# Forget attention and two MLPs on one core: the first eight attention units turn their probabilities by a product with a diagonal of the sums' reciprocals instead of normalising and transposing them

## The chip, the cores and the metric

The kernel runs on one core of a Trainium2 chip. The metric is the device time of one execution in microseconds (us); the median of the runs of the kernel before is 1039.59 us. TensorE is PE in the profile (PEld is its loading of weights), VectorE is DVE, ScalarE is ACT, GpSimd is POOL, and SP issues most of the DMAs.

## The reference

Inputs are q, k, v of shape (4, 8, 576, 64) and gates s of shape (4, 8, 576), all float32. What is computed, cut to what matters:

```python
scores = scale * np.matmul(q, k.transpose(0, 1, 3, 2))
cum = np.cumsum(np.maximum(s, 0.0), axis=-1)
bias = -(cum[:, :, :, None] - cum[:, :, None, :])
scores = np.where(causal, -1000000000.0, scores + np.minimum(bias, 0.0))
attn = np.exp(scores - np.max(scores, axis=-1, keepdims=True))
attn = attn / (np.sum(attn, axis=-1, keepdims=True) + 1e-09)
out = np.matmul(attn, v)                    # 4 x 8 x 576 x 64
x = out.transpose(0, 2, 1, 3).reshape(2304, 512)
h = x @ w_in;  r = max(h, 0);  x = (s * r * r + b) @ w_out         # first MLP, 512 -> 2048 -> 512
h = x @ w_in2; x = (max(h, 0) + alpha * min(h, 0)) @ w_out2        # second MLP
```

## The kernel before

The attention is cut into 32 units: a batch, a pair of heads, and a range of queries. A unit of range 0 has queries 0 to 320 in three blocks of 64, 128 and 128 rows (numbers 0, 1, 2); a unit of range 1 has queries 320 to 576 in two blocks of 128 (3, 4). The order is batch, range, pair, so units 0 to 3 are batch 0, range 0, and units 4 to 7 are batch 0, range 1. Names carry batch, pair and range: `sc_3_0_0_0_1` is a score of unit (0, 0, 1), which is unit 4.

For each head of a unit, `scores` (L402) makes the biased scores of each block, takes the row maximum (L459), and lets ACT do the exponential with the row sums `sm` (L471). Then DVE adds 1e-9 to the sums and takes reciprocals (L478, L479), and POOL multiplies each block's probabilities by them, in place (L482). `values` then turns the probabilities: for every 128 keys and every block that reaches them PE transposes a 128x128 piece into a PSUM bank `pt` (L513), 6 pieces for a head of range 0 and 9 for one of range 1. ACT or DVE copies the bank into SBUF (`pf`, L517), PE multiplies it with v (`av`, L529), and ACT copies the result into the MLP's input (`xf`, L544).

The first eight units are `native`: their scores and value products run in plain float32, where one product is two PE records over its columns. Later units split each operand in two and use the faster fp32r type.

The first MLP runs in seven blocks of 256 tokens and one of 512, each of 16 steps over slices of the hidden size: `up` (L781), ReLU and square on ACT (L800, L802), a split into a high part by ACT and a low part by POOL or DVE (L130, L131), and `down` (L895). Block 0 needs the outputs of units 0 to 3, block 1 those of units 4 to 7. So the program has an early stage, in which units 0 to 3 run with weight slices that are fetched and converted beside them (L140 to L142, L130, L131; `wt`, `w`), and PE fills gaps with products of a zero tile (`busy`, L97), and then a stage in which the units are interleaved with the MLP's steps. After the first MLP comes the second.

The order on each engine is not written by hand: a scheduler places every instruction when the program is built, by its own estimate of durations, and each engine then runs its list in order. Tiles of one tag share a slot; a new tile of that tag waits until the slot's last reader is done. The tags `xs0` and `xs1` have one slot each, and before the change unit 8 is the first to use them.

Of the kernel before, what the change touches and what calls it, by code (L numbers as in the profile page):

```python
# [8 lines left out]
F32 = mybir.dt.float32  # L9
# [3 lines left out]
AF = mybir.ActivationFunctionType  # L13
ALU = mybir.AluOpType
# [5 lines left out]
def tile_forget_attention__then__two_mlps(  # L20
# [20 lines left out]
    nc = tc.nc  # L41
    B, H, S, D = q.shape
    NT, DM = out.shape
    DFF = w_in1.shape[1] // 2
    P = 128
    NP = H // 2
# [5 lines left out]
    IB = [(0, 64)] + [(64 + 128 * n, 192 + 128 * n) for n in range(4)]  # L52
    R1 = IB[2][1]
    QK = S - R1 + S
    EARLY, NATIVE = NP, 2 * NP

# [8 lines left out]
    one = ctx.enter_context(tc.tile_pool(name="one", bufs=1))  # L67
# [12 lines left out]
    ident = const.tile([P, P], F32, name="ident")  # L80
# [13 lines left out]
    def busy(n):  # L94

        for _ in range(n):
            tc.keep_in_program_order(nc.tensor.matmul(scratch, dense[:, :P], dense, start=True, stop=True))  # L97
# [31 lines left out]
    def split(hi, lo, src, lo_eng=nc.vector):  # L129
        nc.scalar.copy(hi, src)  # L130
        lo_eng.tensor_tensor(out=lo, in0=src, in1=hi.bitcast(F32), op=ALU.subtract)  # L131
# [36 lines left out]
    for f in range(len(SPARE), NF):  # L168
        at = int((f - len(SPARE)) * PACE)
# [106 lines left out]
    class Unit:  # L276
        def __init__(self, n):
            self.n = n
            self.b, self.pr, self.rng = units[n]
            self.tag = "_".join(str(i) for i in units[n])  # L280
            self.h0 = 2 * self.pr
            self.blocks = (0, 1, 2) if self.rng == 0 else (3, 4)
            self.q0, self.q1 = (0, R1) if self.rng == 0 else (R1, S)
            self.nv = 3 if self.rng == 0 else 4
            self.probs = [None, None]

            self.early = 0 < n < EARLY
            self.native = n < NATIVE
            self.n_banks = 0
            self.cums = []  # L290

# [110 lines left out]
    def scores(u, h):  # L402

        own = HALF[h]
        head = u.b * H + u.h0 + h
        flip = u.native and h == 1
        nr = len(u.blocks)
        nm = two.tile([P, 3], F32, tag="nm", name=f"nm_{u.tag}_{h}")
        sm = two.tile([P, 3], F32, tag="sm", name=f"sm_{u.tag}_{h}")
        if u.rng == 0:  # L410
            nc.gpsimd.memset(sm[:, 0:1], 1.0)
        big = None if u.early else two.tile([P, 1088], F32, tag="probs", name=f"probs_{u.tag}_{h}")
        probs, col = {}, 0
        for r in u.blocks:
            i0, i1 = IB[r]
            rows = i1 - i0
            if u.early and r != 1:
                big, col = u.buf(two, 0, F32, "", f"probs{h}{r}"), 0

            width = -(-i1 // P) * P if i1 < S else S  # L420
            pt = probs[r] = big[:, col : col + width]
            col += width
            if width > i1:
                nc.gpsimd.memset(pt[:, i1:], 0.0)
            if r == 0:
                nc.gpsimd.memset(pt[64:P, 0:64], 0.0)

            if flip:
                nc.scalar.activation(
                    pt[:rows, :i1], u.cums[h][:rows, :i1], AF.Relu, scale=-1.0, bias=cumT[:rows, r, head : head + 1]  # L430
                )
            else:
                nc.vector.tensor_scalar(
                    out=pt[:rows, :i1], in0=u.cums[h][:rows, :i1], scalar1=cumT[:rows, r, head : head + 1],
                    scalar2=0.0, op0=ALU.subtract, op1=ALU.min,
                )
            nc.gpsimd.affine_select(
                out=pt[:rows, i0:i1], in_=pt[:rows, i0:i1], pattern=[[-1, rows]], base=0,
                channel_multiplier=1, compare_op=ALU.is_ge,
                fill=-MASKED if flip else MASKED,  # L440
            )
        u.probs[h] = probs
        for m, r in enumerate(u.blocks):
            i0, i1 = IB[r]
            rows, n = i1 - i0, i1
            a0 = i0 - u.q0
            pt = probs[r]
            init = -KEEP_ALL if flip else KEEP_ALL
            for j0, j1 in ([(0, n)] if n <= 512 else [(0, 320), (320, n)]):
                sc = u.bank("sc", f"sc{h}_{r}_{j0}")  # L450

                scr, all_ = sc[:rows, : j1 - j0], sc[:, : j1 - j0]
                aq = slice(a0, a0 + P)
                if u.native:
                    nc.tensor.matmul(all_, u.qk[0][own, aq], u.qk[1][own, j0:j1], start=True, stop=True)
                else:
                    nc.tensor.matmul(all_, u.xs[h][0][:, aq], u.xs[h][1][:, j0:j1], start=True, stop=False)
                    nc.tensor.matmul(all_, u.ql[h][:, aq], u.xs[h][1][:, j0:j1], start=False, stop=True)  # L458
                nc.vector.tensor_tensor_reduce(  # L459
                    out=pt[:rows, j0:j1], in0=scr, in1=pt[:rows, j0:j1], scale=SCALE if flip else -SCALE, scalar=init,  # L460
                    op0=ALU.subtract if flip else ALU.add, op1=ALU.max if flip else ALU.min,
                    accum_out=nm[:rows, m : m + 1],
                )
                if u.n < EARLY:
                    busy(1)
                init = nm[:rows, m : m + 1]
            if flip:
                nc.vector.tensor_scalar(
                    out=nm[:rows, m : m + 1], in0=nm[:rows, m : m + 1], scalar1=-1.0, scalar2=None, op0=ALU.mult
                )  # L470
            nc.scalar.activation(  # L471
                pt[:rows, :n], pt[:rows, :n], AF.Exp, bias=nm[:rows, m : m + 1], scale=1.0 if flip else -1.0,
                accum_out=sm[:rows, m : m + 1],
            )
            yield
        if u.n == 0:
            busy(4)
        nc.vector.tensor_scalar(out=sm[:, :nr], in0=sm[:, :nr], scalar1=1e-9, scalar2=None, op0=ALU.add)  # L478
        nc.vector.reciprocal(sm[:, :nr], sm[:, :nr])  # L479
        for m, r in enumerate(u.blocks):  # L480
            rows, n = IB[r][1] - IB[r][0], IB[r][1]
            nc.gpsimd.tensor_scalar(  # L482
                out=probs[r][:rows, :n], in0=probs[r][:rows, :n], scalar1=sm[:rows, m : m + 1],
                scalar2=1.0, op0=ALU.mult, op1=ALU.mult,
            )
        yield

    def values(u, h):
# [10 lines left out]
        for n_bank, bank in enumerate(banks):  # L499
            f0, fn = bank[0][1], bank[-1][1] + width[bank[-1][0]]  # L500
            tp = u.bank("tr", f"pt{h}_{n_bank}")
            moves = []
            for c, off in bank:
                for r in u.blocks:
                    i0, i1 = IB[r]
                    if P * c >= i1:
                        continue

                    partial = r and P * c > i0
                    o = off + i0 - max(q0, P * c)  # L510
                    moves.append((not partial, -c if partial else o, o, r, min(P * c, S - P)))
            for _, _, o, r, k0 in sorted(moves):
                nc.tensor.transpose(tp[:, o : o + P], u.probs[h][r][:, k0 : k0 + P], ident)  # L513
            n_p = (2 * h + n_bank) % 2
            if u.native:
                pf = two.tile([P, 512], F32, tag=("ph", "pl")[n_p], name=f"pf_{u.tag}_{h}_{n_bank}")
                (nc.scalar.copy, nc.vector.tensor_copy)[n_p](pf[:, f0:fn], tp[:, f0:fn])  # L517
                parts = (pf,)
            else:
                ph = two.tile([P, 512], F32R, tag="ph", name=f"ph_{u.tag}_{h}_{n_bank}")  # L520
                pl = two.tile([P, 512], F32R, tag="pl", name=f"pl_{u.tag}_{h}_{n_bank}")
                split(ph[:, f0:fn], pl[:, f0:fn], tp[:, f0:fn])
                parts = (ph, pl)
            yield
            for z, part in enumerate(parts):
                for c, o in bank:
                    w = width[c]
                    lhs = (u.vn if u.native else u.vs[h])[:, c].rearrange("p z d -> p (z d)")
                    nc.tensor.matmul(  # L529
                        av[:, nq - w : nq], lhs, part[:, o : o + w],  # L530
                        start=(c == 0 and z == 0), stop=(c == last_c and z == len(parts) - 1),
                        skip_group_check=True,
                    )
# [451 lines left out]
    for n in range(len(BLOCKS) * NF):  # L985
# [20 lines left out]
        for j in range(NF):  # L1006
            at = LAG[0] + int((j - len(SPARE)) * PACE) if j >= len(SPARE) else j
# [46 lines left out]
```

## Time and profile before

| | us |
|---|---|
| median of three runs | 1039.59 |
| the three runs | 1043.21, 1039.59, 1036.9 |
| profiled execution, its own time | 1039.36 |
| profiled execution, span from first to last instruction | 1037.6 |
| first MLP product (`up`, L781) starts at | 58.68 |

The profiled execution spent 1.76 us outside its span. The rows from it stand below; times in them count from the span's start. A busy PE in such a row includes the tails of pipelined matmuls, so that PE's speed is read from the distance between starts. A group's mean mixes undisturbed and delayed instructions.

### The profile page before, as it was taken

Reading aid. Unit: us, or ns where it says so; the run is one execution under the profiler, and the core shown is the slowest. Engines: PE = TensorE matmul, PEld = TensorE weight load, DVE = VectorE, ACT = ScalarE, POOL = GpSimd, SP = SyncE. Lnnn points to the kernel's source line nnn. Section 1 sums busy time; section 2 is a strip of 40 time slices with the busy share of each in tenths; the row PEclk is TensorE's granted clock in tenths of the full one; section 3 lists DMA queues with packets and bytes.
Section 4 is the critical chain, followed back from the end, with each engine's and each line's share of the span. In section 5 each row is a group of like instructions: output and inputs, shape, how many; then the busy total and the mean of one; then the engine's idle time right before and its main releaser. Section 6 shows DMA issues by size and latency. Waiting matters only on the chain. (4 is left out here: it accounts for less than half of the span.)

```text
span 1037.6 us, 20643 instructions
## 1 busy us (share of the span) xinstructions
PE 1018.5 (98%) x6949; PEld 925.5 (89%) x6952; DVE 674.4 (65%) x1605; ACT 670.7 (65%) x1668; POOL 450.6 (43%) x876
## 2 busy tenths in 40 slices
PE   9999999999999999999999999999999999999997
PEld 4578899999999999999999888888999999999996
DVE  6899665687677766677655865857665456455443
ACT  5878766777787877878776776645554454445433
POOL 5555675666677576777562000574611011001000
PEclk9899999999999999999999999999999999999999
DMA  7997443343143432324215762645644335334331
GB/s 150 257 249 223 120 76 68 73 98 76 40 89 67 99 72 52 82 65 91 68 34 177 230 199 78 205 148 176 200 154 142 102 114 171 103 102 133 105 102 48
DMA packets 197930, 125.45 MB, mean 121 GB/s; under 512 B 138496, under 2 KB 167936, under 8 KB 197824
## 3 DMA queue, kind: packets, MB, share of 16 engines
q1 hardware_dynamic: 193744, 123.56, 42.8%
q8 instruction: 55, 0.90, 0.4%
q10 hardware_dynamic: 4080, 0.57, 0.3%
q14 instruction: 51, 0.42, 0.1%
HBM read 106.19 MB, written 17.90 MB: 120 GB/s over the span
## 5 line engine op out<-in xcount | busy, mean ns | idle before, releaser
L781 PE MATMUL hp<-xh,w 128*128 128x256 f32 (+1 forms) x1024 | 229.9, 301 | 1.1 <-ACT r L800 1.1
L905 PE MATMUL acc<-w,ring 128*128 128x512 f32 x864 | 214.6, 392 | 1.1 <-DVE ring L131 0.7
L905 PEld LDWEIGHTS acc<-w,ring 128*128 128x128 f32 x864 | 155.9, 188 | 29.4 <-DVE ring L131 1.1
L781 PEld LDWEIGHTS hp<-xh,w 128*128 128x128 f32 x1024 | 171.4, 189 | 9.3 <-ACT r L800 1.4
L895 PE MATMUL acc<-gh,w 128*128 128x256 f32 x896 | 170.3, 286 | 0.4 <-ACT res L924 0.4
L781 PE MATMUL hp<-xl,w 128*128 128x256 f32 (+1 forms) x512 | 152.3, 298 | 0.0
L895 PEld LDWEIGHTS acc<-gh,w 128*128 128x128 f32 x896 | 135.3, 189 | 2.4 <-ACT res L924 1.0
L881 POOL TENSOR_TENSOR cc<-u,t 128x256 f32<-128x256 f32 x32 | 26.9, 839 | 237.2 <-DVE u L872 202.9
L895 PE MATMUL acc<-gl,w 128*128 128x256 f32 x448 | 117.7, 288 | 1.4 <-POOL gl L131 1.4
L482 POOL TENSOR_SCALAR probs<-probs,sm 64x64 f32<-64x64 f32 (+4 forms) x160 | 89.2, 571 | 58.9 <-DVE sm L479 51.9
L471 ACT ACTIVATE probs<-probs,nm 64x64 f32<-64x64 f32 (+4 forms) x160 | 89.9, 562 | 35.8 <-DVE nm L459 26.9
L131 POOL TENSOR_TENSOR gl<-r,gh 128x256 fp32r<-128x256 f32 x112 | 87.7, 784 | 51.3 <-ACT gh L130 41.4
L815 PE MATMUL p<-xs,sums 128*128 128x256 f32 x768 | 104.6, 282 | 0.4 <-DVE u L857 0.4
L815 PEld LDWEIGHTS p<-xs,sums 128*128 128x128 f32 x768 | 98.0, 189 | 2.0 <-DVE u L857 0.6
L781 PEld LDWEIGHTS hp<-xl,w 128*128 128x128 f32 x512 | 97.1, 190 | 2.7
L459 DVE CUSTOM_DVE_ANT_0 probs<-sc,probs 128x320 f32<-128x320 f32 (+3 forms) x160 | 68.4, 428 | 42.1 <-PE sc L458 28.8
L815 PEld LDWEIGHTS p<-xs,w 128*128 128x128 f32 x576 | 79.0, 189 | 8.4 <-DVE u L872 1.7
L800 ACT ACTIVATE r<-hp 128x256 f32<-128x256 f32 (+1 forms) x144 | 58.0, 403 | 43.7 <-PE hp L781 31.6
L815 PE MATMUL p<-xs,w 128*128 128x256 f32 x576 | 82.0, 282 | 2.3 <-DVE u L872 1.5
L895 PEld LDWEIGHTS acc<-gl,w 128*128 128x128 f32 x448 | 79.8, 189 | 2.5 <-POOL gl L131 1.9
L513 PE MATMUL pt<-ident,probs 128*128 128x128 f32 x480 | 75.3, 275 | 3.1 <-POOL probs L482 2.7
L826 DVE SCALAR_TENSOR_TENSOR ph<-pl,misc,ph 128x512 f32<-128x512 f32 x64 | 50.6, 790 | 42.3 <-ACT pl L842 42.3
(151 smaller groups left out, 2104.3 us busy)
## 6 DMA issues: line engine op xcount, KB each, us to landing
sums<-sums_d SPq DMA_DIRECT2D x128, 256.0 KB, 2.7
wi<-in_moe_w_in_dram SPq DMA_DIRECT2D x32, 512.0 KB, 5.0
wo<-in_moe_w_out_dram SPq DMA_DIRECT2D x32, 512.0 KB, 5.1
cum<-cum_d SPq DMA_DIRECT2D x32, 288.0 KB, 3.6
sums_d<-w SPq DMA_DIRECT2D x64, 128.0 KB, 1.9
cum<-cum_d SPq DMA_DIRECT2D x30, 160.0 KB, 3.0
nat<-in_k_dram SPq DMA_DIRECT2D x64, 72.0 KB, 2.5
x_d<-res SPq DMA_DIRECT2D x18, 256.0 KB, 2.4
```

Source lines behind the costliest of these rows:

```text
L131: lo_eng.tensor_tensor(out=lo, in0=src, in1=hi.bitcast(F32), op=ALU.subtract)
L459: nc.vector.tensor_tensor_reduce(out=pt[:rows, j0:j1], in0=scr, in1=pt[:rows, j0:j1], scale=SCALE if flip else -SCALE, scalar=init, op0=AL ...
L471: nc.scalar.activation(pt[:rows, :n], pt[:rows, :n], AF.Exp, bias=nm[:rows, m : m + 1], scale=1.0 if flip else -1.0, accum_out=sm[:rows, m ...
L482: nc.gpsimd.tensor_scalar(out=probs[r][:rows, :n], in0=probs[r][:rows, :n], scalar1=sm[:rows, m : m + 1], scalar2=1.0, op0=ALU.mult, op1=A ...
L513: nc.tensor.transpose(tp[:, o : o + P], u.probs[h][r][:, k0 : k0 + P], ident)
L781: nc.tensor.matmul(hs, a[:, c], b[c], start=(n == 0), stop=(n == len(terms) * NCC - 1))
L800: relus.append(nc.scalar.activation(r, hs, AF.Relu, scale=1.0 / W_SCALE).ins)
L815: nc.tensor.matmul(bank, lhs[:, c * P : (c + 1) * P], rhs[:, c], start=(start and c == 0 and z == 0), stop=(c == 1 and z == 2), skip_group ...
L826: nc.vector.scalar_tensor_tensor(out=r, in0=u, scalar=nalpha[:, f : f + 1], in1=r, op0=ALU.mult, op1=ALU.add).ins
L881: nc.gpsimd.tensor_tensor(out=cc[:, T:], in0=u3, in1=t5, op=ALU.add)
L895: nc.tensor.matmul(banks[d] if count == 2 else acc[d // 2][:, d % 2], a[:, d * P : (d + 1) * P], b, start=(f == 0 and (d % 2 == 0 or count ...
L905: nc.tensor.matmul(banks[m], a[:, m * P : (m + 1) * P], b, start=(f == 0 and b is woh and a is gh), stop=(f == NF - 1 and a is gl),)
```

## The change

For units 0 to 7 the pass of L482 is gone. In its place a 128x128 float32 diagonal of the reciprocals is made for each block, in a tile of the tag `xs0` (first head, made by ACT: the identity times the row's reciprocal) or `xs1` (second head, made by DVE). The transposition becomes an ordinary float32 product of the probabilities, as weights, with that diagonal, as the moving operand, which turns and scales at once. Its columns are cut to those that are needed: 64, 128, 128, 64, 128 and 64 for a head of range 0 (576 in all), and seven times 128 and twice 64 for a head of range 1 (1024). A clearing of 64 rows of block 0 on POOL (L426) falls away too. Units 8 to 31 are as before.

```diff
-    EARLY, NATIVE = NP, 2 * NP
+    EARLY, NATIVE, SPREAD = NP, 2 * NP, 8
...
+            self.spread = n < SPREAD
+            self.diag = [None, None]
...
-            if r == 0:
+            if r == 0 and not u.spread:
                 nc.gpsimd.memset(pt[64:P, 0:64], 0.0)
...
+        if u.spread:
+            u.diag[h] = one.tile([P, QK], F32, tag=f"xs{h}", name=f"diag{h}_{u.tag}")
         for m, r in enumerate(u.blocks):
             rows, n = IB[r][1] - IB[r][0], IB[r][1]
+            if u.spread:
+                turn = u.diag[h][:rows, m * P : m * P + rows]
+                if h:
+                    nc.vector.tensor_scalar(
+                        out=turn, in0=ident[:rows, :rows], scalar1=sm[:rows, m : m + 1], scalar2=None, op0=ALU.mult
+                    )
+                else:
+                    nc.scalar.activation(turn, ident[:rows, :rows], AF.Copy, scale=sm[:rows, m : m + 1])
+                continue
             nc.gpsimd.tensor_scalar(
...
-            for _, _, o, r, k0 in sorted(moves):
+                    moves.append((not partial, -c if partial else o, o, r, min(P * c, S - P), max(0, P * c - i0)))
+            for _, _, o, r, k0, skip in sorted(moves):
+                if u.spread:
+                    rows = IB[r][1] - IB[r][0]
+                    at = (r - u.blocks[0]) * P
+                    nc.tensor.matmul(
+                        tp[:, o + skip : o + rows], u.probs[h][r][:rows, k0 : k0 + P],
+                        u.diag[h][:rows, at + skip : at + rows], start=True, stop=True,
+                    )
+                    continue
                 nc.tensor.transpose(tp[:, o : o + P], u.probs[h][r][:, k0 : k0 + P], ident)
```

In the changed kernel's file the lines behind the first addition stand 2 to 21 lower. ACT's list before, at the end of the early stage (`pf_0_3_0_1_0` is the turned bank of unit 3's second head, the last that block 0 waits for; `xh0_0` is the high part of block 0's input; `r0_0` is its first ReLU):

```order
L517 COPY pf_0_3_0_1_0_838<-pt1_0_0_3_0_832 128x512
L130 CAST w0_4_2_18_914<-wt0_4_1_906 128x512
L544 COPY xf0_433<-av1_0_3_0_831 64x256
L544 COPY xf1_435<-av1_0_3_0_831 64x64
L471 ACTIVATE probs_0_0_1_1_924,sm_0_0_1_1_923<-probs_0_0_1_1_924,nm_0_0_1_1_922 128x448
L130 CAST xh0_0_869<-xf0_433 128x256
L517 COPY pf_0_0_1_0_0_945<-pt0_0_0_0_1_940 128x512
L800 ACTIVATE r0_0_896<-hp0_0_0_881 128x256
```

The same place in the changed kernel:

```order
L473 ACTIVATE probs_0_0_1_1_925,sm_0_0_1_1_924<-probs_0_0_1_1_925,nm_0_0_1_1_923 128x448
L493 ACTIVATE diag0_0_0_1_855<-ident_85,sm_0_0_1_0_816 128x128 x2
L538 COPY pf_0_3_0_1_0_838<-pt1_0_0_3_0_832 128x512
L130 CAST w0_4_2_18_915<-wt0_4_1_907 128x512
L538 COPY pf_0_0_1_0_0_946<-pt0_0_0_0_1_941 128x512
L565 COPY xf0_432<-av1_0_3_0_831 64x256
L565 COPY xf1_434<-av1_0_3_0_831 64x64
L473 ACTIVATE probs_0_0_1_1_925,sm_0_0_1_1_924<-probs_0_0_1_1_925,nm_0_0_1_1_923 128x576
L130 CAST xh0_0_870<-xf0_432 128x256
L821 ACTIVATE r0_0_897<-hp0_0_0_882 128x256
```

The two diagonals of unit 4's first head have come ahead of `pf_0_3_0_1_0`, and unit 4's next copy and its last exponential ahead of `xh0_0`.

PE's list before, where block 0 begins (the turning of unit 4's first head, `pt_0_0_0_1` and `pt_1_0_0_1`, stands among the products of `up`):

```order
L781 MATMUL hp_0_0_881<-xh_0_869,w_0_0_63_205 128x256
L513 MATMUL pt_0_0_0_1_940<-ident,probs_0_1_0_817 128x128
L455 MATMUL sc_4_0_0_0_1_947<-turned_0_1_695 128x320
L455 MATMUL sc_4_320_0_0_1_950<-turned_0_1_695 128x256
L513 MATMUL pt_0_0_0_1_940<-ident,probs_0_1_0_817 128x128 x3
L781 MATMUL hp_0_0_881<-xh_0_869,w_0_0_0_204 128x256
L781 MATMUL hp_0_0_881<-xl_0_870,w_0_0_0_204 128x256
L781 MATMUL hp_0_0_881<-xh_0_869,w_0_0_63_205 128x256
L513 MATMUL pt_1_0_0_1_957<-ident,probs_0_1_0_817 128x128 x5
L529 MATMUL av_0_0_1_939<-pf_0_1_0_0_945,vn_0_1_577 128x256 x2
```

The same place in the changed kernel:

```order
L529 MATMUL pt_0_0_0_1_941<-diag_0_0_1_855,probs_0_1_0_817 128x128 x3
L550 MATMUL av_0_3_0_831<-pf_3_0_1_0_838,vn_3_0_223 128x320
L550 MATMUL av_0_3_0_831<-pf_3_0_1_0_838,vn_3_0_223 128x192
L550 MATMUL av_0_3_0_831<-pf_3_0_1_1_851,vn_3_0_223 128x64
L97 LDWEIGHTS dense
L97 MATMUL acc_first_96<-dense 128x512
L802 MATMUL hp_0_0_882<-xh_0_870,w_0_0_0_204 128x256
...
L802 MATMUL hp_0_0_882<-xh_0_870,w_0_0_63_205 128x256
L529 MATMUL pt_1_0_0_1_958<-diag_0_0_1_855,probs_0_1_0_817 128x64 x2
L529 MATMUL pt_1_0_0_1_958<-diag_0_0_1_855,probs_0_1_0_817 128x128 x3
```

The first bank of unit 4's first head is now turned ahead of block 0's first product; all other turning of units 4 to 7 stays among the MLP's products.

## Rows read from the trace of the kernel before

**Rows 1.** The page, section 1: busy time of each engine over the span.

```profile
PE 1018.5 (98%) x6949; PEld 925.5 (89%) x6952; DVE 674.4 (65%) x1605; ACT 670.7 (65%) x1668; POOL 450.6 (43%) x876
```

**Rows 2.** Busy time by stretches; the first row names the columns.

```profile
core 0: us, PE busy (x) PEld busy (x) DVE busy (x) ACT busy (x) POOL busy (x), PEclk, DMA share, GB/s
20.00:58.68 38.68, 34.17 (x147) 20.40 (x148) 34.28 (x110) 30.45 (x87) 22.39 (x49) 0.91 0.93 241
58.68:122.00 63.32, 63.00 (x418) 53.16 (x416) 54.49 (x117) 51.74 (x125) 36.94 (x54) 1.00 0.77 210
```

**Rows 3.** Waits of PE, 58.68 to 122 us: total, times, longest.

```profile
PE av L529 <- DMA vn<-in_v_dram: 0.3, 1, 0.3
```

**Rows 4.** Waits of DVE, 20 to 58.68 us: total, times, longest.

```profile
DVE wt L141 <- ACT wt L140: 1.9, 2, 1.2
DVE pf L517 <- PE pt L513: 1.3, 1, 1.3
DVE probs L459 <- PE sc L455: 0.9, 2, 0.6
```

**Rows 5.** Timeline of PE in block 0: start, time, instruction, tile, shape, records.

```profile
62.05 0.71 PE L513 MATMUL pt<-ident,probs 128*128 128x128 f32 x5
...
66.08 1.09 PE L529 MATMUL av<-pf,vn 128*128 128x256 f32 x6
66.98 0.72 PE L895 MATMUL acc<-gh,w 128*128 128x256 f32 x4
```

**Rows 6.** Source line 513, 0 to 145 us: durations in ns as min/median/max.

```profile
L513 PE MATMUL pt<-ident,probs x120: 270/273/477, 15.9 to 139.1; 128*128 128x128 f32 x120
```

**Rows 7.** Source line 482, 0 to 145 us: instructions, what they wait for, who waits.

```profile
L482 POOL TENSOR_SCALAR probs<-probs,sm x43: 312/528/1267, 12.7 to 143.7; 64x64 f32<-64x64 f32 x9, 128x192 f32<-128x192 f32 x9, 128x320 f32<-128x320 f32 x9, 128x448 f32<-128x448 f32 x8
...
  DVE sm L479: 14.8, 10
...
  PEld pt L513: 5.1, 8
  PE pt L513: 2.7, 4
```

**Rows 8.** Groups by form, ACT, 0 to 145 us: count, busy us, mean ns.

```profile
L429 ACT ACTIVATE probs<-cum,cumT 128x192 f32<-128x192 f32 x3 | 1.3, 439 | 0.0
L429 ACT ACTIVATE probs<-cum,cumT 64x64 f32<-64x64 f32 x3 | 1.0, 348 | 4.5 <-DMA cum<-cum_d 4.5
```

**Rows 9.** Timeline of DVE, early stage.

```profile
13.76 0.98 DVE L433 TENSOR_SCALAR probs<-cum,cumT 64x64 f32<-64x64 f32 x3 [0.61 <-DMA cum<-cum_d]
...
22.79 1.65 DVE L433 TENSOR_SCALAR probs<-cum,cumT 64x64 f32<-64x64 f32 x3
...
33.14 0.91 DVE L141 TENSOR_SCALAR wt<-wt 128x512 uint32<-128x512 uint32 x1 [0.68 <-ACT wt L140]
...
41.84 0.40 DVE L131 TENSOR_TENSOR xl<-xf,xh 128x256 fp32r<-128x256 f32 x1
...
44.07 0.41 DVE L141 TENSOR_SCALAR wt<-wt 128x512 uint32<-128x512 uint32 x1
...
53.03 1.14 DVE L131 TENSOR_TENSOR xl<-xf,xh 128x256 fp32r<-128x256 f32 x1
```

**Rows 10.** Timeline of POOL, early stage.

```profile
22.73 1.53 POOL L482 TENSOR_SCALAR probs<-probs,sm 64x64 f32<-64x64 f32 x3 [0.71 <-DVE sm L479]
...
32.54 1.22 POOL L482 TENSOR_SCALAR probs<-probs,sm 64x64 f32<-64x64 f32 x3 [2.53 <-DVE nm L468]
...
36.96 1.27 POOL L131 TENSOR_TENSOR w<-wt,w 128x512 fp32r<-128x512 f32 x1
...
52.64 1.22 POOL L482 TENSOR_SCALAR probs<-probs,sm 64x64 f32<-64x64 f32 x3 [0.16 <-DVE pf L517]
```

**Rows 11.** Busy time from 36 to 42.6 us, columns as in group 2.

```profile
36.00:42.60 6.60, 6.25 (x16) 3.89 (x17) 5.85 (x20) 5.98 (x19) 2.75 (x6) 0.51 0.68 161
```

More of the change, by code (lines that the diff above doesn't have):

```diff
@@ L510, in values @@
                     o = off + i0 - max(q0, P * c)
-                    moves.append((not partial, -c if partial else o, o, r, min(P * c, S - P)))
-            for _, _, o, r, k0 in sorted(moves):
+                    moves.append((not partial, -c if partial else o, o, r, min(P * c, S - P), max(0, P * c - i0)))
[8 more added lines that the diff above has]
+                    continue
                 nc.tensor.transpose(tp[:, o : o + P], u.probs[h][r][:, k0 : k0 + P], ident)
```

## The prediction, made before the changed kernel ran

> **What bounds the kernel now.** I read the page's busy times first [rows 1]: PE is busy for 98% of the span, no other engine for more than 65%, so whatever lengthens PE's own work looks costly. But that share is a mean. Cut at the first product of the MLP, 58.68 us, it falls into two parts [rows 2]. From 58.68 to 122 us, where units 4 to 7 run among the steps of block 0, PE is busy for 63.00 of 63.32 us, and its listed waits there come to 0.3 us [rows 3]: PE sets the time. From 20 to 58.68 us PE's busy 34.17 of 38.68 us flatters it, because it holds products of a zero tile and half-speed stretches; there DVE is the fullest engine with useful work, 34.28 us, and its waits add up to 1.9 + 1.3 + 0.9 = 4.1 us [rows 2, 4]. ACT has 30.45 us. So the early stage is set by DVE and ACT handing work to each other, and the rest by PE. The change works in both, and I cost them apart.
>
> **PE's added work.** A transposition: five records take 0.71 us, one alone 0.273, so (0.71 - 0.273) / 4 = 0.109 us from start to start [rows 5, 6]. A float32 product over 128 columns does not occur before, but the value products beside it are the same kind: six records, 256 + 192 + 64 = 512 columns, start at 66.08 and the next instruction at 66.98 [rows 5]. That is 0.90 us, 1.76 ns a column in float32, with the changes of weights in it.
>
> - A head of range 1: before 9 x 0.109 = 0.98 us; after 1024 x 1.76 ns = 1.80 us; 0.82 us more.
> - A head of range 0: before 6 x 0.109 = 0.65 us; after 576 x 1.76 ns = 1.01 us; 0.36 us more.
>
> Units 4 to 7 have eight heads of range 1, all turned behind 58.68 us before: 8 x 0.82 = 6.6 us. In the new order one bank of the first head stands ahead of block 0's first product; its 4 products, 0.9 us, come off the PE-bound stage, which so grows by 5.7 us. PE has no wait there to hide it in. Bounds: if short products need more for their weights, 64 columns could cost what 128 do, 2 of 9 products by 0.11 us each, 1.8 us more; if nothing is lost between products, each of a product's two records over 128 columns takes as long as a transposition, 0.218 us for both, and the stage grows by 8 x (8 x 0.218 - 0.98) - 0.9 = 5.2 us. I keep 5.2 to 7.5 us. The eight heads of range 0 add 8 x 0.36 = 2.9 us to PE in the early stage, where it has room; what counts there is 0.36 us more in the chain of each head.
>
> **The early stage: what goes.** POOL's pass ran 43 times up to 145 us, of which 40 belong to the first eight units; three in a row take 1.22 us undisturbed [rows 7, 10]. PE waited for it 12 times, 5.1 + 2.7 = 7.8 us [rows 7]. That is the most that the shorter chain can give back, and it gives less, since DVE, not PE, was the fuller engine: DVE's only wait that leads to it is `pf` for `pt`, 1.3 us [rows 4]. Second, DVE is slower while POOL runs: three biases (L433) take 0.98 us alone and 1.65 beside POOL's pass at 22.73; L141 takes 0.41 alone and 0.91 beside the pass at 32.54; a subtraction takes 0.40 alone and 1.14 beside the pass at 52.64 [rows 9, 10]. These three are 0.67 + 0.50 + 0.74 = 1.9 us; I allow up to twice that for the passes not shown, and take 2.5 us.
>
> The Trainium skill ("SBUF — State Buffer", section "SBUF: two separate sides") says that VectorE in a two-port mode, or with two SBUF inputs, and GpSimd share one port pair, and that whichever starts first holds it for its whole instruction. The trace agrees in the three cases above. The rule cuts both ways: the relief is real, but the new diagonals on DVE can be shut out by POOL's other work. By it the sum would move by the rival on POOL below; the sum here goes by the rows.
>
> **What comes.** DVE makes 3 diagonals for each second head of units 0 to 3, 12 in all. Three biases of 64, 192 and 320 columns take 0.98 us [rows 9], and the diagonals are 64, 128 and 128 columns: at most 0.98 us a head, hardly less than half of it; I take 0.6, so 2.4 us. DVE's account is then even: 2.4 us in, 2.5 us out. ACT makes 12 for the first heads, and 2 for unit 4, which the order puts straight ahead of the copy that block 0 waits for. ACT's biases take 348 ns for 64 columns and 439 for 192 [rows 8]; 128 columns lie between, at 0.39 us by the line through both; from below only the slope holds, 0.09 us for 128 columns. I take 0.3, near the row, since neighbours in a list can overlap: 14 x 0.3 = 4.2 us (1.3 to 5.5) on an engine that had 38.68 - 30.45 = 8.2 us free in this stage, part of it at the start where little is ready. In addition the order has brought unit 4's copy and last exponential ahead of `xh0_0`. Behind a diagonal on ACT stand conversions of weights, exponentials and `pf` copies. POOL waited 14.8 us in 10 pieces for the reciprocals [rows 7], which cost nothing as little was queued behind; ACT would pay for such a wait, but the scheduler puts several instructions between a head's last exponential and its diagonals. I take 1 us as the net lengthening of the early stage by ACT, less 0.5 us for the shorter chain: +0.5 us, with bounds of -8 us (all of PE's waits for POOL) and +5.5 us (every diagonal of ACT on the path, at its dearest).
>
> **Costed at nothing.** In block 0, DVE gains 8 diagonals (units 4 to 7, about 1.8 us) and ACT 6 more (1.8 us), on engines busy 54.49 and 51.74 of 63.32 us [rows 2], while PE paces. If that cover failed, they would add up to 2 us. Unit 8's tiles of the tags `xs0` and `xs1` wait for unit 7's diagonals; units 8 to 11 feed block 2, a whole block later.
>
> **Sum.** 1039.4 (the profiled execution's own time, 0.2 below the median of the runs) + 5.7 + 0.5 = 1045.6, rounded to 1046 us.
>
> **Rivals.**
>
> *The early stage gives it back (no change).* For it: 7.8 us of PE's waits for POOL, and DVE's delays. The clock may help: from 36 to 42.6 us it stood at 0.51 of full speed, the lower level of 1.2 GHz, PE having been fed with gaps [rows 11]; more float32 products could close them, for about the 1.3 us wait of DVE that follows. Against: DVE and ACT take over the work. If 1.5 to 8 us come back, the time is 1037 to 1044 us.
>
> *ACT or POOL's port on the path (slower still).* The diagonals of ACT all count, +4.2 to 5.5, or the four groups of DVE each meet one of POOL's long subtractions, 1.27 us [rows 10], 4 x 1.27 = 5.1 us. The time is 1039.4 + 5.7 + 4.2 to 5.5, 1049 to 1051 us.
>
> *Faster.* One mechanism, the release of the early stage from POOL: PE's 7.8 us and DVE's relief at its upper bound, 3.8 us, would both have to shorten the stage in full. That is 11.6 us against 5.7 us: 1033.5 us. It decides only if the stage shrinks by more than 5.7 + 5.2 = 10.9 us, from 58.7 to under 47.8 us. Rows 4 speak against it, with DVE idle for only 4.1 us of it.
>
> That the change does not do what it says is not among them: the order shows the products in the place of the transpositions, and no pass of L482 for units 0 to 7.
>
> **How the numbers follow.** This kernel's measurement can tell about 0.5%, 5.2 us, from no change: faster means under 1034.4, slower above 1044.8 us. The forecast case (PE's work counts, the early stage about as long) has 0.48, 1043.5 to 1048 us, most of it above the line: 0.43 slower, 0.05 no change. The early stage giving it back: 0.30, no change. The path through ACT or POOL's port: 0.13, slower. Faster: 0.07. The last 0.02 I count as slower. So slower 0.58, no change 0.35, faster 0.07. The range leaves out the faster case, the low end of the second and the high end of the third: 1038 to 1051 us.
>
> **What would show it.** Right: the products of units 4 to 7 take about 1.8 us a head where transpositions took 1.0, PE stays without waits from its first MLP product on, and the end of block 0 moves later by 5 to 7 us against that first product. The first product itself lies within 1 or 2 us of 58.7 us. DVE's biases show fewer doubled times, and ACT is busier by some 4 us before that point. Wrong: the first product comes before 54 us, which means that POOL's pass and not DVE and ACT held the early stage; or PE's added work is met by shorter gaps between its records in block 0, so that block 0 does not lengthen; or ACT stands waiting for reciprocals in front of its diagonals, and block 0 begins after 61 us.

## The result, and the profile after

The changed kernel takes 1051.82 us (median of six runs, 1050.65 to 1054.32) against 1037.74 us (six runs) of the kernel before: ratio 1.0127, 95% interval 1.0108 to 1.0146. It is slower, as forecast, by 14.1 us where 6.6 were forecast (1039.4 to 1046), and it lies just above the range's upper end of 1051. The profiled execution took 1054.32 us, its span 1052.5, 14.9 us more than the span before.

The page's busy times, answering to [rows 1]: PE is still the full engine, with 123 records more. (The change adds 120; runs 7 and 8 below, with the matmuls of the kernel before, have 6952, so three are missing from the trace before.)

```profile
PE 1035.3 (98%) x7072; PEld 943.6 (90%) x7072; DVE 667.7 (63%) x1625; ACT 678.8 (64%) x1688; POOL 428.2 (41%) x828
```

The next rows are busy times by stretches of the changed kernel, columns as in [rows 2]: the early stage up to the first `up` product (now L802), which starts at 70.10 us instead of 58.68, and blocks 0, 1 and 2 of the MLP, each from its first product to that of the next.

```profile
20.00:70.10 50.10, 45.38 (x206) 31.50 (x205) 34.48 (x130) 35.30 (x100) 13.36 (x28) 0.86 0.83 220
70.10:163.90 93.80, 93.80 (x653) 82.47 (x652) 70.36 (x175) 72.42 (x180) 44.67 (x85) 1.00 0.57 144
163.90:236.20 72.30, 71.41 (x567) 69.56 (x566) 46.14 (x144) 53.40 (x146) 47.84 (x107) 1.00 0.37 77
236.20:305.20 69.00, 69.00 (x578) 68.71 (x578) 44.29 (x129) 51.42 (x132) 43.74 (x83) 1.00 0.29 63
```

The same three blocks of the kernel before, which had no rows above:

```profile
58.70:144.40 85.70, 85.12 (x575) 73.37 (x573) 68.86 (x161) 67.74 (x168) 52.49 (x91) 1.00 0.66 172
144.40:218.80 74.40, 73.24 (x580) 71.03 (x578) 47.68 (x151) 53.52 (x151) 47.97 (x114) 1.00 0.35 74
218.80:290.70 71.90, 70.50 (x585) 69.67 (x583) 51.88 (x137) 53.47 (x136) 45.88 (x88) 1.00 0.31 69
```

The reader is to see where the 14.9 us lie: 11.4 in the early stage, 8.1 in block 0, 5.0 given back in blocks 1 and 2 (2.1 and 2.9), 0.4 in the 747 us behind them. In the early stage a ledger can be made from the first row and from [rows 2]. PE stood for 50.10 - 45.38 = 4.7 us (before 4.5). A mean granted clock of 0.86 of full speed loses 0.14 x 50.10 = 7.0 us (before 0.09 x 38.68 = 3.5). What is left is PE's work at full speed: 38.4 us (before 30.7). So the 11.4 us are 7.7 of work, 3.5 of clock, 0.2 of standing. The clock column has two digits, which is good to some 0.3 us. The split between work and clock is rougher, because time in which PE stood at the lower clock is charged to the clock as well: run 4 below needs 40.7 us at full clock for its 207 records in this stage, where the ledger gives the changed kernel 38.4 for 206. So the clock can be charged some 2 us too much.

Where PE stood longest is in the list of waits of the changed kernel, 20 to 70.1 us (total, times, longest), a line of PE and a line of ACT:

```profile
PE pt L529 <- ACT diag L493: 2.8, 1, 2.8
...
ACT probs L431 <- DMA cum<-cum_d: 3.8, 2, 3.5
```

The timelines show how the two hang together: DVE's reciprocals of unit 1's first head, ACT's list, and PE's.

```profile
24.74 0.16 DVE L481 RECIPROCAL sm<-sm 128x3 f32<-128x3 f32 x1
```

```profile
24.95 0.56 ACT L538 COPY pf<-pt 128x512 f32<-128x512 f32 x1
29.02 1.15 ACT L431 ACTIVATE probs<-cum,cumT 64x64 f32<-64x64 f32 x3 [3.51 <-DMA cum<-cum_d]
30.07 0.60 ACT L130 CAST w<-wt 128x512 fp32r<-128x512 f32 x1
30.58 0.93 ACT L493 ACTIVATE diag<-ident,sm 64x64 f32<-64x64 f32 x3
```

```profile
27.71 0.43 PE L550 MATMUL av<-pf,vn 128*128 128x64 f32 x2 [1.02 <-DVE pf L538]
27.98 0.59 PE L97 MATMUL acc_first<-dense 128*128 128x512 bf16 x2
31.36 1.39 PE L529 MATMUL pt<-diag,probs 128*128 128x64 f32 x6 [2.78 <-ACT diag L493]
```

The reciprocals were there at 24.90. The diagonals began at 30.58, because in ACT's list the biases of unit 3's second head (L431) stand ahead of them, and those waited for the load of their cumulative gates (`cum`) until 29.02. In the kernel before the same load held ACT too [rows 8], but unit 1's pass ran on POOL, at 22.73 [rows 10], and its turning began at 23.96:

```profile
23.96 0.79 PE L513 MATMUL pt<-ident,probs 128*128 128x128 f32 x5
```

In the changed kernel it begins 7.4 us later. Behind PE's wait stand the scores of unit 2, and the clock fell. Busy times by 5 us of the changed kernel, columns as in [rows 2]:

```profile
25.00:30.00 5.00, 2.07 (x9) 1.05 (x8) 2.17 (x10) 1.49 (x5) 2.42 (x10) 1.00 1.01 268
30.00:35.00 5.00, 3.64 (x11) 2.09 (x11) 1.48 (x5) 4.80 (x16) 2.07 (x6) 0.72 0.90 246
35.00:40.00 5.00, 4.58 (x15) 2.91 (x13) 2.89 (x15) 2.98 (x7) 0.10 (x1) 0.50 0.82 205
40.00:45.00 5.00, 5.00 (x18) 4.00 (x18) 3.74 (x8) 3.53 (x12) 1.55 (x2) 0.50 1.03 261
45.00:50.00 5.00, 5.00 (x26) 3.36 (x25) 3.40 (x15) 4.25 (x12) 1.15 (x1) 0.91 1.00 218
```

PE was busy for 2.07 of 5 us, and from there the granted clock went to 0.50, the level of 1.2 GHz, for about twice as long as before.

### The profile page after: what moved, and what is told of

It is laid out like the page before. It is cut to its first block, busy times and chain, and to the rows that moved or that the text cites. A ratio compares the mean times of both kernels' runs of the same rounds, so it can differ in the third digit from the quotient of the medians.

```text
span 1052.5 us, 20884 instructions
## 1 busy us (share of the span) xinstructions
PE 1035.3 (98%) x7072; PEld 943.6 (90%) x7072; DVE 667.7 (63%) x1625; ACT 678.8 (64%) x1688; POOL 428.2 (41%) x828
## 5 line engine op out<-in xcount | busy, mean ns | idle before, releaser
L802 PE MATMUL hp<-xh,w 128*128 128x256 f32 (+1 forms) x1024 | 230.1, 301 | 0.0
L802 PEld LDWEIGHTS hp<-xh,w 128*128 128x128 f32 x1024 | 171.5, 190 | 8.1 <-issue 2.1
L802 PE MATMUL hp<-xl,w 128*128 128x256 f32 (+1 forms) x512 | 152.7, 298 | 0.0
L802 PEld LDWEIGHTS hp<-xl,w 128*128 128x128 f32 x512 | 97.1, 190 | 2.8
L495 POOL TENSOR_SCALAR probs<-probs,sm 128x448 f32<-128x448 f32 (+3 forms) x120 | 66.3, 565 | 35.0 <-DVE sm L481 34.1
L847 DVE SCALAR_TENSOR_TENSOR ph<-pl,misc,ph 128x512 f32<-128x512 f32 x64 | 51.1, 798 | 42.7 <-ACT pl L863 42.7
L568 DVE TENSOR_TENSOR xf<-av,xf 64x128 f32<-64x128 f32 (+3 forms) x88 | 28.0, 318 | 72.6 <-ACT xf L567 72.3
```

The costliest lines, as they stand in the source:

```text
L495: nc.gpsimd.tensor_scalar(out=probs[r][:rows, :n], in0=probs[r][:rows, :n], scalar1=sm[:rows, m : m + 1], scalar2=1.0, op0=ALU.mult, op1=A ...
L568: nc.vector.tensor_tensor(out=dst, in0=src, in1=dst, op=ALU.add)
L802: nc.tensor.matmul(hs, a[:, c], b[c], start=(n == 0), stop=(n == len(terms) * NCC - 1))
L847: nc.vector.scalar_tensor_tensor(out=r, in0=u, scalar=nalpha[:, f : f + 1], in1=r, op0=ALU.mult, op1=ALU.add).ins
```

## The experiments

Four theories: **the wait** (a load that ACT waits for stands ahead of its diagonals), **the products** (a float32 product costs PE more than the forecast said, in both stages), **the load** (the diagonals' own time on ACT and DVE), and **the clock** (gaps in PE's work halve its clock). All ratios are to the kernel before, run on the same chip. The time of one and the same kernel moves with the clock granted in the run, so intervals are wide where that varies, and the profile of one run is read beside the ratio. The four columns on the right are in us and go by the early stage, 20 us to the first `up` product, as in the ledger above; added dummy products count as PE's work. Run 2 leaves that stage as it was.

| run | ratio, 95% interval | first `up` | PE stood | lost to the clock | PE's work |
|---|---|---|---|---|---|
| before | | 58.68 | 4.5 | 3.5 | 30.7 |
| changed | 1.0127, 1.0108 to 1.0146 | 70.10 | 4.7 | 7.0 | 38.4 |
| 1 units 0 to 3 alone | 1.0059, 1.0046 to 1.0072 | 68.53 | 2.9 | 6.8 | 38.8 |
| 2 units 4 to 7 alone | 1.0086, 1.0073 to 1.0099 | 57.69 | | | |
| 3 unit 1's diagonals on DVE | 1.0139, 1.0110 to 1.0167 | 66.20 | 1.4 | 5.1 | 39.7 |
| 4 all diagonals on POOL | 1.0156, 1.0127 to 1.0185 | 62.69 | 2.0 | 0 | 40.7 |
| 5 pass, product with identity | 1.0100, 1.0076 to 1.0125 | 64.80 | 1.2 | 4.9 | 38.7 |
| 6 no pass, product with identity | 1.0093, 1.0078 to 1.0107 | 61.14 | 0.6 | 0 | 40.6 |
| 7 no pass, transposition | 0.9994, 0.9980 to 1.0007 | 58.14 | 4.1 | 1.5 | 32.5 |
| 8 pass, transposition, idle diagonals | 1.0095, 1.0082 to 1.0108 | 67.46 | 6.7 | 11.9 | 28.9 |
| 9 changed, ten dummy products | 1.0115, 1.0091 to 1.0139 | 67.08 | 2.7 | 3.3 | 41.1 |
| 10 before, eight dummy products | 0.9980, 0.9967 to 0.9993 | 59.49 | 4.1 | 3.6 | 31.8 |
| 11 units 0 to 3 alone, POOL | 1.0038, 1.0013 to 1.0063 | 62.32 | 2.1 | 0 | 40.2 |
| 12 before, fourteen dummy products | 0.9984, 0.9966 to 1.0002 | 59.27 | 1.6 | 3.5 | 34.2 |

**Runs 1 and 2: each stage alone.**

```diff
-            self.spread = n < SPREAD
+            self.spread = n < EARLY              # run 1
+            self.spread = EARLY <= n < SPREAD    # run 2
```

> Only the first four units turn by the product with a diagonal, units 4 to 7 keep POOL's pass and the transposition. All theories: the first `up` product starts at 69 to 71 us, as in the changed kernel (70.1), and not at 58.7. If the early stage alone makes the loss and nothing is given back later, the ratio is 1.010 to 1.012 (10 to 12 us); if what is late at the start is partly given back in blocks 1 and 2, 1.004 to 1.008.

> Only units 4 to 7 turn by the product. The first `up` product stays at 58 to 60 us. By the prediction's sum the block stage gains 5.7 us, ratio 1.0055 (bounds 5.2 to 7.5 us); if the net 3.2 us between the two traces is the true price of the longer products, 1.003; if the whole 8.1 us that block 0 grew by belongs to the products, 1.008.

Run 1: +6.0 us (1044.01 against 1037.97), the first `up` product at 68.53, block 0 85.4 us, and blocks 1 and 2 at 72.7 and 69.1, 4.5 us shorter than before. Run 2: +9.0 us. Together 15.0, where the whole change costs 14.1: the two stages add up. The blocks of run 2:

```profile
57.70:152.20 94.50, 94.50 (x657) 82.82 (x656) 70.02 (x169) 69.78 (x174) 42.70 (x76) 1.00 0.59 155
152.20:226.10 73.90, 71.92 (x569) 69.90 (x568) 49.07 (x151) 54.19 (x151) 47.27 (x112) 1.00 0.36 75
226.10:297.90 71.80, 70.42 (x584) 69.60 (x583) 51.78 (x135) 53.51 (x136) 46.17 (x88) 1.00 0.31 68
```

PE never stands in block 0, at full clock. The three blocks take 240.2 us against 232.0, +8.2, and PE stands in them for 3.4 us where it stood for 3.1. So 72 products cost some 8.0 us more than 72 transpositions, 0.111 us each, and a product is 0.109 + 0.111 = 0.220 us: two records, each as long as a transposition. One bank of run 2 shows it without a difference of sums, three products of 128 columns and two of 64, and the instruction behind them:

```profile
61.55 1.27 PE L529 MATMUL pt<-diag,probs 128*128 128x64 f32 x10
62.66 1.03 PE L550 MATMUL av<-pf,vn 128*128 128x256 f32 x4
```

From start to start these are 1.11 us, 0.222 for a product, where the columns alone (512 by the prediction's 1.76 ns) would give 0.90. Blocks 1 and 2 start 8 us late here and are not shorter, so lateness alone does not shorten them.

**Run 3: the wait on ACT taken away.**

```diff
-                if h:
+                if h or u.n == 1:
                     nc.vector.tensor_scalar(
```

> As the changed kernel, but the three diagonals of unit 1's first head are made on DVE, so that ACT's wait for the load of unit 3's sums no longer stands ahead of them. Theory of the wait (order on ACT): that turning starts at 24 to 26 us instead of 31.4, the first `up` product at 61 to 65 us, the ratio falls to 1.004 to 1.008. Theory of the longer products, or of the load that the diagonals put on ACT and DVE: the first `up` product stays at 69 to 71 us and the ratio at 1.011 to 1.014.

The first `up` product comes at 66.20: 3.9 of the 11.4 us are gone, less than the theory of the wait asked (61 to 65 us). The turning of unit 1 starts at 28.20, not at 24 to 26, and the half clock is still there.

```profile
25.00:30.00 5.00, 4.16 (x21) 2.83 (x21) 3.28 (x15) 2.95 (x7) 4.38 (x16) 1.00 0.89 268
30.00:35.00 5.00, 4.44 (x21) 3.07 (x20) 4.82 (x16) 4.86 (x16) 1.04 (x2) 0.85 1.08 318
35.00:40.00 5.00, 5.00 (x17) 3.85 (x17) 2.85 (x12) 3.36 (x13) 1.39 (x2) 0.50 0.71 157
```

The ratio, for which the theory asked 1.004 to 1.008, did not fall. Its six runs spread from 1046.05 us, at a granted clock of 1.000, to 1056.12 at 0.987. So the wait is real but it is a third of the early loss, and the theory that it is the cause falls.

**Run 4: all diagonals on POOL**, where the pass was.

```diff
-                if h:
-                    nc.vector.tensor_scalar(
...
-                    nc.scalar.activation(turn, ident[:rows, :rows], AF.Copy, scale=sm[:rows, m : m + 1])
+                nc.gpsimd.tensor_scalar(
+                    out=turn, in0=ident[:rows, :rows], scalar1=sm[:rows, m : m + 1],
+                    scalar2=1.0, op0=ALU.mult, op1=ALU.mult,
+                )
```

> As the changed kernel, but all diagonals are made on POOL, where the pass was that they replace; ACT and DVE get none. Theory of the wait on ACT: the first `up` product starts at 58 to 63 us, ratio 1.003 to 1.007, what is left being the longer products. Theory of the longer products alone: 68 to 71 us and 1.011 to 1.014. Theory of the load on ACT and DVE: 58 to 63 us too, and it can be told from the wait by the run with unit 1's diagonals alone on DVE, which leaves that load in place.

The first `up` product comes at 62.69, as the theories of the wait and of the load asked, and in the profiled run the clock holds at 1.00:

```profile
20.00:62.70 42.70, 40.68 (x207) 27.57 (x206) 31.45 (x117) 32.68 (x92) 23.66 (x51) 1.00 0.94 239
```

PE is busy for all but 2.0 us of the stage: with the products in it, PE sets the time here too. The ratio is not the 1.003 to 1.007 that they asked: the whole kernel is no faster than the changed one. Block 0 takes 95.2 us, and two of six runs had a clock of 0.987 to 0.988 (1058 us, against 1049.5 at 0.998).

**Runs 5 to 8: product, pass and diagonals one by one.** Run 5 keeps the pass and makes no diagonals; run 6 leaves out the pass as well; run 7 is the kernel before without its pass; run 8 the kernel before with diagonals that nothing reads. The edits of the turning in runs 5 and 6, and of the loop that normalises in run 8:

```diff
-                        u.diag[h][:rows, at + skip : at + rows], start=True, stop=True,
+                        ident[:rows, skip:rows], start=True, stop=True,
...
                     nc.scalar.activation(turn, ident[:rows, :rows], AF.Copy, scale=sm[:rows, m : m + 1])
-                continue
             nc.gpsimd.tensor_scalar(
```

> POOL's pass that normalises stays, no diagonals are made; only the turning of the first eight units goes by a float32 product with the identity, in the forms of the changed kernel. Theory of the longer products (two records of some 0.115 us in place of one of 0.11, 120 products, 48 of them before the first `up` product): first `up` product at 64 to 70 us, ratio 1.011 to 1.015. Theory that the diagonals (their wait on ACT, their load on ACT and DVE) make the loss: first `up` product at 58 to 62 us, ratio at most 1.008, what the products cost in block 0 alone.

> As the run with the pass and the product with the identity, but the pass is left out too, so that for the first eight units the division by the sums is not computed: what is left is the product's price without pass and without diagonals. Theory of the longer products: still 1.009 to 1.014. Theory of the diagonals: at most 1.008, and less than the run with the pass. The difference to the run with the pass is what the pass costs on the path: 0 to 4 us.

> The kernel before without POOL's pass for the first eight units, so that their division by the sums is not computed; turned by transpositions, no diagonals: the most that removing the pass can bring. If the pass is hidden (PE finds other work): ratio 0.998 to 1.001. If PE's waits for it before the first `up` product (2.7 us on PE, 5.1 us on its weight loads) are on the path: 0.995 to 0.998.

> The kernel before, with pass and transpositions, which also makes the diagonals on ACT and DVE as the changed kernel does; nothing reads them. Theory of the longer products: ratio 0.998 to 1.003, first `up` product at 58 to 60 us. Theory of the load on ACT and DVE: 1.003 to 1.010, first `up` product at 62 to 68 us.

The products alone cost 1.0% with the pass (+9.6 us) and without it (1049.28 against 1038.84 of run 7, +10.4 us): most of the loss, as the theory of the products asked, though run 5 stays just under its range. At equal clock the price is higher still: all four runs of run 6 were at 0.999 or 1.000, and the two of run 7 at 1.000 took 1035.67 and 1035.86 us, some 13 us less; its other ten were at 0.995 to 0.998. The pass costs nothing that can be measured: run 7 is at 0.9994, its first `up` product 0.5 us earlier, although DVE is busy for 4.1 us less in its early stage than in [rows 2]:

```profile
20.00:58.14 38.14, 34.02 (x160) 21.13 (x159) 30.14 (x116) 32.46 (x94) 12.44 (x27) 0.96 0.92 241
```

This is the most that taking the pass away could have brought.

Run 8 is where my table of theories failed. The diagonals, which should have cost at most 3 us by the theory of the products, cost 10 us (1049.19 against 1039.24), as the theory of the load asked, though PE's work is not longer. The early stage of run 8 and of run 6, columns as in [rows 2]:

```profile
20.00:67.46 47.46, 40.80 (x146) 23.68 (x145) 33.42 (x120) 32.68 (x96) 25.26 (x50) 0.75 0.84 219
```

```profile
20.00:61.14 41.14, 40.58 (x211) 28.33 (x210) 31.46 (x120) 33.82 (x97) 12.42 (x28) 1.00 0.92 235
```

PE is busy in this stage of run 8 for 40.80 us with 146 records, where it was busy for 34.17 with 147 before [rows 2]: 6.6 of the 8.8 us by which the stage is longer, at a mean clock of 0.75 instead of 0.91 (by the ledger 11.9 us lost to the clock instead of 3.5). Run 6, with the longer products and nearly no gap, loses nothing to the clock. In run 8 PE waits for the pass for 6.7 us on its matmuls, where it waited 2.7 [rows 7], and POOL's passes are slower beside the busier DVE; three of them:

```profile
20.98 1.21 POOL L494 TENSOR_SCALAR probs<-probs,sm 64x64 f32<-64x64 f32 x3 [3.49 <-DVE nm L470]
...
23.53 2.47 POOL L494 TENSOR_SCALAR probs<-probs,sm 64x64 f32<-64x64 f32 x3
...
34.70 2.97 POOL L494 TENSOR_SCALAR probs<-probs,sm 64x64 f32<-64x64 f32 x3 [3.16 <-DVE nm L470]
```

The first takes 1.21 us, as undisturbed before [rows 10]. The last ran while DVE did its conversions, the diagonals and a subtraction, and took 2.97. So products and diagonals do not add up: about 10 us each apart, 14.1 together, probably since the longer products also fill gaps that let the clock fall; no run takes this apart.

**Run 9: the clock, with ACT's order left alone.**

```diff
             tp = u.bank("tr", f"pt{h}_{n_bank}")
+            if (u.n, h, n_bank) == (1, 0, 0):
+                busy(10)
```

> The changed kernel with ten more of the dense dummy products that it already uses, ahead of the turning of unit 1's first head, where PE stood waiting for ACT's diagonals (2.8 us, and 2.1 us busy in the 5 us before). ACT's order and its wait are unchanged. If the half clock of 13.65 us after that gap comes from PE having stood, the half clock shrinks to at most 7 us, the first `up` product starts at 65 to 68 us and the ratio falls to 1.006 to 1.010. If the clock falls whatever PE does there, the first `up` product stays at 70 to 72 us and the ratio at 1.012 to 1.015.

The first `up` product comes at 67.08 instead of 70.10, in the range expected, and 3.3 us are lost to the clock instead of 7.0:

```profile
20.00:67.08 47.08, 44.35 (x216) 30.23 (x215) 35.36 (x130) 35.07 (x101) 12.87 (x28) 0.93 0.86 235
```

Two rows of PE's timeline show that the wait itself did not get shorter:

```profile
28.92 4.01 PE L97 MATMUL acc_first<-dense 128*128 128x512 bf16 x12
32.77 1.11 PE L531 MATMUL pt<-diag,probs 128*128 128x64 f32 x6
```

Unit 1's turning starts 1.4 us later than in the changed kernel (31.36), behind twelve dummy products, and the stage ends 3.0 us earlier. That speaks for the clock. The ratio, 1.0115, is above the 1.006 to 1.010 that were expected, and its interval overlaps that of the changed kernel: it does not settle the matter.

**Runs 10 and 12: the same in the kernel before; run 11: the products in the early stage alone, without a load on ACT and DVE.** Run 10 puts two dummy products ahead of each turning of units 1 and 2; run 12 has six more ahead of the wait that took their place.

```diff
+            if 0 < u.n < 3 and n_bank == 0:     # runs 10 and 12
+                busy(2)
...
-                    busy(1)
+                    busy(7 if (u.n, h, r) == (3, 1, 2) else 1)    # run 12
```

> The kernel before with two more dummy products ahead of the turning of each head of units 1 and 2, where PE waits for POOL's pass. If the 6.8 us at half clock in the kernel before come from these gaps: clock 0.999 to 1.000 in all runs, first `up` product at 55 to 57.5 us, ratio 0.996 to 0.999. If the gaps have nothing to do with it, or the eight dummy products (about 2 us) cost more than they give back: 1.000 to 1.003.

> Products with diagonals in the first four units alone, where PE is not always busy, with all diagonals made on POOL; units 4 to 7 keep pass and transposition. By the runs so far: first `up` product at 61 to 64 us, block 0 at 85 to 86 us as before, blocks 1 and 2 together 4 to 5 us shorter, as in the run with the early units alone: ratio 0.997 to 1.003. If the shorter blocks 1 and 2 were only the lateness given back, nothing is won: 1.002 to 1.006.

> The kernel before with the eight dummy products of the run before, and six more after unit 3's last scores, ahead of the turning that waited 1.33 us for POOL there, after which the clock fell to half for some 7 us. If the half clock comes from PE having stood there: clock 0.999 to 1.000, first `up` product at 56 to 58 us, ratio 0.994 to 0.997. If a gap elsewhere takes its place, or the gaps have nothing to do with it: clock 0.995 to 0.998 as before, ratio 0.998 to 1.001.

Run 10 is a miss in its mechanism: 3.6 us are lost to the clock as before, now behind a wait of 1.33 us at 46.24, and the stage is 0.8 us longer. It is nevertheless faster by 0.2%, less than the half per cent that a measurement of this kernel tells well. Its blocks 0 to 2:

```profile
59.50:147.30 87.80, 87.80 (x593) 74.78 (x592) 75.36 (x173) 70.78 (x176) 53.90 (x99) 1.00 0.67 170
147.30:219.50 72.20, 71.42 (x567) 69.59 (x566) 47.12 (x147) 53.71 (x148) 48.48 (x108) 1.00 0.37 77
219.50:288.60 69.10, 69.10 (x579) 68.81 (x579) 44.35 (x130) 51.48 (x132) 43.83 (x83) 1.00 0.29 65
```

Blocks 1 and 2 are as short as in the changed kernel, with neither a product with a diagonal nor a late start. What the changed kernel got back there comes from the order that the scheduler made: PE stands for 0.8 us in the three blocks instead of 3.1, and part of the work lies in block 0. Run 12, with the same short blocks 1 and 2, is at 0.9984 and misses its range too. Its profiled run lost 3.5 us to the clock again, not behind the wait that was filled but between 35 and 45 us, where the kernel before loses it as well [rows 11]; its runs at a clock of 1.000 took 1033.0 to 1034.4 us, those at 0.991 took 1041.6. Run 11 has a stage at full clock, a first `up` product at 62.32 and blocks 1 and 2 together 4.0 us shorter, as expected; at clocks of 0.998 and 0.999 it takes 1038 to 1041 us, about as before, but six of its twelve runs, at 0.995 or less (1041 to 1048.6 us), bring the ratio to 1.0038, above the range. No version beats the kernel before by half a per cent.

## Why the prediction was right in its sign and too low

**What bounds the kernel.** For block 0 this held: PE stood there for 0.6 us before and not at all after, and what was added to its work came out at the end. For the early stage it did not. That "the early stage is set by DVE and ACT handing work to each other" does not fit run 7, where DVE is busy for 4.1 us less and the stage is only 0.5 us shorter. The sentence built on it, that the heads of range 0 add to PE "in the early stage, where it has room", is the first step that failed. PE's 4.5 us of standing were spread over waits and its dummy products stay in the order, so the room was not used: it stands for 4.7 us after the change. In runs 4 and 6, where little else holds PE, its work fills 40.7 of 42.7 us and 40.6 of 41.1. By the ledger its work grew by 7.7 us: 42 of the 48 products lie behind 20 us, by 0.111 they are 4.7; four products of unit 4 are another 0.9, and part of unit 4's scores is now ahead of the first `up` product as well. The rest is within what the ledger can tell.

**PE's added work, 5.7 us.** Right mechanism, a term of the wrong size. The product was charged by columns, 1024 x 1.76 ns = 1.80 us a head. Run 2 gives 9 x 0.220 = 1.98 us, as if the two products of 64 columns cost what the others do, which the prediction kept as its upper bound. So 8.0 us for the eight heads instead of 6.6; in the changed kernel block 0 grew by 8.1 us, above the upper bound of 7.5, although four of the products had left it. The 5.0 us that came back in blocks 1 and 2 were not foreseen at all; the three blocks grew by 3.1 us net.

**The pass.** That taking it away gives back far less than PE's 7.8 us of waits was right: run 7 gives 0.5 us of the early stage and nothing measurable at the end. With it the rivals "gives it back" and "faster" had no ground in the pass. The 7.8 us were read too high besides: 5.1 of them are waits of weight loads, which run beside PE's own 2.7, and PE stood in that stage for 4.5 us in all. DVE's relief was real and larger than the 2.5 us forecast: with as many instructions as before, the biases (L433, now L435) took 4.1 us instead of 7.7 up to the first `up` product, L141 3.4 instead of 4.3 and the subtractions for `xl` 1.2 instead of 2.2. None of it shortened the stage, since DVE did not set it.

**The diagonals.** Their own times were well judged: three in a row took ACT 0.93 us, 0.31 each (forecast 0.3), and DVE 0.63 us a head (forecast 0.6). Their place was not. The prediction held that the scheduler puts several instructions between an exponential and its diagonals, so that ACT would not wait. It did, and three of these instructions waited 3.5 us for a load. This is the second failed step. The sign that the prediction named for itself (ACT waiting in front of its diagonals, block 0 after 61 us) was seen, with a load in the place of the reciprocals; by run 3 this is worth 3.9 us of the stage.

**The clock.** The prediction thought of it only as a gain: products could close the gaps behind which it fell. Runs 4, 6 and 11 show that, with nothing lost in the early stage of their profiled runs, though other runs of 4 and 11 were at clocks down to 0.987 and 0.988. In the changed kernel the diagonals opened other gaps, and by the ledger the loss doubled from 3.5 to 7.0 us. The stage's term of +0.5 us, with an upper bound of 5.5, held neither this nor PE's work; it measured 11.4.

**The nearest rival.** "ACT or POOL's port on the path", 1049 to 1051 us, came closest to the time, and ACT was on the path. But its price was ACT's own time for the diagonals, 4.2 to 5.5 us; what was paid was a wait behind a load, PE's longer work and the clock, less the 5.0 us that came back. That these make nearly the same sum is luck.

**The rival on POOL's port.** Its cost was looked for on DVE, whose diagonals took no longer than forecast. Run 8, which keeps the pass, shows a cost on the other side: POOL's passes at 2.47 and 2.97 us against 1.21. The Trainium skill ("SBUF — State Buffer", section "SBUF: two separate sides") says that VectorE in a two-port mode, or with two SBUF inputs, and GpSimd share one port pair and that the one that starts first holds it for its whole instruction. The trace agrees as far as POOL's passes are longer beside VectorE's work; which instruction held the ports it does not show.

What stays open: why one and the same kernel is granted clocks from 0.987 to 1.000 in different runs, and which of the gaps in a run decides it. And the share of the order made by the scheduler in the 5.0 us of blocks 1 and 2 is shown by runs 10 and 12, not taken apart.

## What to carry to other kernels

Price a float32 product by its records: here 64 columns saved hardly anything against 128, and each cost two transpositions, so a pass on a half-idle engine (POOL, 43% busy) was exchanged for work on the one that is 98% busy. When an operation moves to another engine's list, read what stands ahead of it there, loads above all, not only how long it takes. And before calling an engine idle in a stage, subtract from its time both the waits that cannot be filled and the stretches at the lower clock.

## What the runs showed of the hardware that was not expected

- A float32 product of 128 rows and up to 128 columns took 0.220 us on average at full clock, two records of the 0.109 us of a transposition.
- After 5 us in which PE was busy for 2.07, the granted clock fell to 0.50 for over 10 us, although PE was then busy for 4.58 and 5.00 of each 5 us. With PE busy for 40.58 of 41.14 us (run 6) it did not fall, and the four runs of that kernel were at 0.999 or 1.000.
- The same kernel's time follows the clock of the run: 1033.0 us at 1.000 and 1041.6 at 0.991 (run 12), 1046.05 at 1.000 and 1056.12 at 0.987 (run 3).
- Diagonals that nothing read cost 10 us (run 8). In the early stage PE was busy for 40.80 us with 146 records, at a mean granted clock of 0.75, where the kernel before had 34.17 us, 147 records and 0.91.
